# Feed forward's first batch: the low parts of weights and activations made by VectorE, between its decoding, with no work for GpSimd

## The chip, the core and the metric

The kernel runs on one core of a Trainium2 chip. The metric is the device time of one execution in microseconds. In this document TensorE does matrix products, VectorE and ScalarE work element by element, GpSimd is a fourth compute engine, and SyncE's queue (SP in the rows) starts the transfers from and to memory. In the rows they are called PE (PEld for its weight loads), DVE, ACT, POOL and SP.

## What is computed

Attention over 4 batches of 448 tokens with 12 heads, with a mixing of the heads before and behind the softmax; a feed forward of 768 to 2048 to 768; and then a layer of eight experts of which each token takes one. Cut to what matters here, the feed forward:

```python
def _moe_ref(x, w_in, w_out):            # x: 1792 x 768, w_in: 768 x 2048, w_out: 2048 x 768
    h = x @ w_in
    g = h * (1.0 / (1.0 + np.exp(-1.702 * h)))
    return (g @ w_out).astype(np.float32)
```

## The kernel before

TensorE multiplies numbers of a shortened format. To keep the accuracy of float32, each operand is split in two: a high part, the number rounded to that format, and a low part, the number less its high part. A product then takes three matmuls: high by high, high by low, low by high. ScalarE makes the high parts with a copy that rounds, and another engine makes the low parts with one subtraction.

The feed forward is the function `moe1`. It has 64 steps: 4 batches of tokens (b), and for each of them 16 slices (f) of 128 hidden columns. For a step the first layer (`l1`, line 268) runs 18 matmuls of 128x448, six blocks with three products each; the activation follows (`act`: tanh on ScalarE at line 273, then one instruction of VectorE at line 274; `act2`: the rounding copy on ScalarE at line 277 and the subtraction at line 278); and the second layer (`l2`, line 285) runs 18 matmuls that add to six sums.

The weights arrive in a form that VectorE has to decode first (`decode`, lines 251 to 254: four instructions of 128x768 for each tile of weights, with ScalarE's absolute value at line 246 for the last of them). The decoded weights stay in the core's memory, so decoding happens only in the first batch, two tiles in each of its steps 0 to 12 and one in step 13. The split of the weights (`split_w`, line 259 on ScalarE and line 260) is made anew for every batch.

The order of the instructions on every engine is the order of the program text. One step s of the loop issues, in this order: `act` of step s+1, `split_w` of the first layer's weights of s+2, `act2` of s+1, `split_w` of the second layer's weights of s+1, the decoding of the two tiles for the next step's splits, `l1` of s+2, and `l2` of s. In the middle of the decoding, behind each of its two instructions at line 253, the load of a tile for two steps later is issued; the very last load has one step. The buffers of the activations (`g`) are one for odd and one for even steps.

Which engine makes a low part: at line 260 GpSimd in the first batch and VectorE in the others, unless the caller names one; at line 278 always GpSimd. Some of the first steps' work (the list `EARLY`) is issued beside the end of the attention stage and names its engine itself. Between its steps the first batch also issues small setup instructions, most of them on GpSimd (`env.setup`, lines 444 to 459).

Of the kernel before, what the change touches and what calls it, by code (L numbers as in the profile page):

```python
# [6 lines left out]
F32 = mybir.dt.float32  # L7
# [4 lines left out]
ALU = mybir.AluOpType  # L12
# [188 lines left out]
def moe1(tc, env, x_in, w_in, w_out, wg):  # L201

    nc=env.nc; NF=FF//128; NE=5
    with ExitStack() as ctx, ExitStack() as late:
# [35 lines left out]
        def wtile(s,z):  # L240
            WS[s,z]=env.wsp.tile([128,2,DM],F32R,tag="ws",bufs=5,name="ws")
# [13 lines left out]
        def split_w(s,z,e=None):  # L255
            b,f=steps[s]; r=WR[f,z]
            if (s,z) not in WS: wtile(s,z)
            t=WS[s,z]
            nc.scalar.copy(t[:,0,:],r)  # L259
            (e or (nc.gpsimd if b==0 else nc.vector)).tensor_tensor(out=t[:,1,:],in0=r,in1=t[:,0,:].bitcast(F32),op=ALU.subtract)  # L260
        PSL={}
        def l1(s):
            b,f=steps[s]; ps=pl.tile([128,512],F32,tag="h",name="psh"); PSL[s]=ps; t=WS.pop((s,0))
# [11 lines left out]
        def act2(s):  # L275
            th=TH.pop(s)
            nc.scalar.copy(G[s][:,0,:],th)  # L277
            nc.gpsimd.tensor_tensor(out=G[s][:,1,:],in0=th,in1=G[s][:,0,:].bitcast(F32),op=ALU.subtract)  # L278
        def l2(s,between=lambda o:None):
            b,f=steps[s]; t=WS.pop((s,1)); g=G.pop(s)  # L280
            if f==0: OB[b]=[L.po.tile([128,512],F32,tag=f"o{o}",name=f"pso{o}") for o in range(6)]
            for i,o in enumerate((2,3,4,5,0,1)):
                between(i); c=slice(o*128,o*128+128)
                for k,(wz,xz) in enumerate(((0,0),(0,1),(1,0))):
                    nc.tensor.matmul(OB[b][o][:,:TB],t[:,wz,c],g[:,xz,:],start=f==0 and k==0,stop=f==NF-1 and k==2)  # L285
# [68 lines left out]
        def dk(*ks):  # L354
# [3 lines left out]
            if 3 in ks: nd[0]+=1  # L358
        A=lambda i: absd(*order[i])
        step={'a':lambda i: absd(*order[i]),'d':dk,'x':lambda c,e: split_x(0,c,EN[e]),'w':lambda s,z,e: split_w(s,z,EN[e]),'l':l1,'t':act,'u':act2}  # L360
        at=0; did=set()
        for t,k,a in EARLY:
# [11 lines left out]
        if ('u',0) not in did: act2(0)  # L374
        for s in range(NS):
            b,f=steps[s]
            if s+1<NS and ('t',s+1) not in did: act(s+1)
            if s+2<NS and ('w',s+2,0) not in did: split_w(s+2,0)
            if b>0 and f==0: evac(b-1)
            if s+1<NS and ('u',s+1) not in did: act2(s+1)  # L380
            if s+1<NS and ('w',s+1,1) not in did: split_w(s+1,1)
# [475 lines left out]
```

## Time and profile before

| | us |
|---|---|
| median of 3 runs | 1334.84 |
| the runs | 1334.59 to 1337.12 |
| the profiled execution | 1341.98 |
| span of the profiled execution | 1340.3 |

| over the span | busy us | share |
|---|---|---|
| TensorE | 1217.9 | 91% |
| VectorE | 787.0 | 59% |
| ScalarE | 606.5 | 45% |
| GpSimd | 312.7 | 23% |

The profile is that of one execution, and its times count from the start of its span. The shares are means over stages that differ: the attention fills about the first 470 us, the first batch of the feed forward lies between about 470 and 625 us, its other batches end at about 991 us, and the experts follow. The profiled execution takes 7.14 us more than the median of the runs, so a difference is worked out within the profile and then taken from the median.

### The profile page before, as it was taken

What the parts mean: (1) busy time and instruction counts of PE and PEld (TensorE: products, weight loads), DVE (VectorE), ACT (ScalarE), POOL (GpSimd) and SP (SyncE); (2) the same over time, 40 slices, a digit from 0 to 9 for tenths busy, and PEclk for the clock granted to TensorE, in tenths of its full rate; (3) what the DMA queues carried; (4) which work ended last, traced back from release to release, by engine and by line L of the source; (5) the groups of instructions that cost most, each with busy time, mean ns of one, the idle gap of its engine ahead of it and who ended that gap; (6) DMA issues with size and microseconds to landing.
All of it is one profiled execution on the core that took longest, in us unless ns stands there. A gap on an engine that the chain in (4) does not pass through costs nothing. (4 is left out here: it accounts for less than half of the span.)

```text
span 1340.3 us, 31619 instructions
## 1 busy us (share of the span) xinstructions
PE 1217.9 (91%) x13086; PEld 992.6 (74%) x13087; DVE 787.0 (59%) x1340; ACT 606.5 (45%) x1203; POOL 312.7 (23%) x385
## 2 busy tenths in 40 slices
PE   7798998898888788779999999999996979999996
PEld 2355555555555577668899899989996979999996
DVE  1565665565655799997543544454437645566663
ACT  2455555555554444434434433443334534445552
POOL 0111111111111555553121112112113202321110
PEclk9899999999999798989999999999997989999998
DMA  7887987987966355420100010000555756656500
GB/s 222 254 242 208 296 239 212 269 254 202 281 186 203 128 203 194 152 96 26 42 22 21 1 52 11 21 1 11 183 198 172 207 160 190 190 198 228 187 20 21
DMA packets 97825, 201.09 MB, mean 150 GB/s; under 512 B 29711, under 2 KB 67733, under 8 KB 97292
## 3 DMA queue, kind: packets, MB, share of 16 engines
q1 hardware_dynamic: 91596, 186.84, 45.4%
q0 software_dynamic: 6080, 12.18, 2.9%
q8 instruction: 104, 1.70, 0.5%
q14 instruction: 45, 0.37, 0.1%
HBM read 143.60 MB, written 56.43 MB: 149 GB/s over the span
## 5 line engine op out<-in xcount | busy, mean ns | idle before, releaser
L268 PE MATMUL psh<-x,ws 128*128 128x448 f32 x1152 | 264.1, 382 | 25.2 <-POOL ws L260 14.9
L268 PEld LDWEIGHTS psh<-x,ws 128*128 128x128 f32 x1152 | 224.5, 197 | 56.0 <-POOL ws L260 20.3
L285 PE MATMUL pso<-g,ws 128*128 128x448 f32 x1152 | 252.7, 369 | 0.0
L285 PEld LDWEIGHTS pso<-g,ws 128*128 128x128 f32 x1152 | 213.8, 188 | 20.1
L135 PEld LDWEIGHTS psa<-M,E 60*64 60x64 f32 x5760 | 98.2, 138 | 115.2 <-POOL M L126 103.7
L119 ACT ACTIVATE E<-psm,st 124x448 f32<-124x448 f32 x180 | 112.5, 629 | 127.3 <-DVE st L116 127.2
L126 POOL TENSOR_SCALAR M<-wq,st 124x60 f32<-124x60 f32 x180 | 78.7, 451 | 354.8 <-DVE st L123 270.1
L260 DVE TENSOR_TENSOR ws<-res,ws 128x768 fp32r<-128x768 f32 x81 | 91.4, 1128 | 105.8 <-ACT ws L259 102.8
L135 PE MATMUL psa<-M,E 60*64 60x60 f32 x5760 | 108.9, 224 | 48.7 <-POOL M L126 43.1
L278 POOL TENSOR_TENSOR g<-th,g 128x448 fp32r<-128x448 f32 x64 | 78.4, 1225 | 308.2 <-ACT g L277 308.1
L661 PE MATMUL psh<-xt,ws 128*128 128x256 f32 (+2 forms) x1152 | 147.7, 289 | 0.1
L661 PEld LDWEIGHTS psh<-xt,ws 128*128 128x128 f32 x1152 | 145.3, 190 | 0.3 <-DVE xt L653 0.3
L628 DVE TENSOR_TENSOR ws<-res,ws 128x768 fp32r<-128x768 f32 x128 | 121.9, 959 | 39.7 <-ACT ws L627 39.5
L143 DVE COPY AT<-psa 128x480 f32<-128x480 f32 x88 | 60.2, 685 | 133.1 <-ACT AT L142 133.1
L89 PE MATMUL psq<-K,Q 64*120 64x448 f32 (+1 forms) x384 | 114.8, 648 | 11.9 <-ACT so L94 7.0
L116 DVE TENSOR_REDUCE st<-psm 124x1 f32<-124x448 f32 x180 | 103.7, 617 | 14.6 <-PE psm L112 13.8
L680 PE MATMUL psy<-ws,hh 128*128 128x384 f32 x576 | 110.4, 345 | 0.0
L627 ACT CAST ws<-res 128x768 fp32r<-128x768 f32 x128 | 105.5, 832 | 7.9 <-PE psy L697 4.9
L259 ACT CAST ws<-res 128x768 fp32r<-128x768 f32 x108 | 89.9, 832 | 35.5 <-DVE res L254 35.5
L151 PE MATMUL psv<-AT,V 128*64 128x120 f32 (+1 forms) x1536 | 98.8, 273 | 6.9 <-DVE X L155 3.5
L680 PEld LDWEIGHTS psy<-ws,hh 128*128 128x128 f32 x576 | 100.9, 190 | 0.0
L112 PE MATMUL psm<-G,wp 60*64 60x448 f32 x720 | 94.5, 578 | 0.5 <-ACT E L119 0.5
(178 smaller groups left out, 1289.5 us busy)
## 6 DMA issues: line engine op xcount, KB each, us to landing
res<-in_wm SPq DMA_DIRECT2D x56, 768.0 KB
G<-S SPq DMA_DIRECT2D x176, 210.0 KB
S<-so SPq DMA_DIRECT2D x72, 420.0 KB
wd<-in_w_in SPq DMA_DIRECT2D x10, 768.0 KB
wd<-in_w_out SPq DMA_DIRECT2D x10, 768.0 KB
S<-so SPq DMA_DIRECT2D x24, 308.0 KB
V<-in_vT SPq DMA_DIRECT2D x16, 384.0 KB
K<-in_kT SPq DMA_DIRECT2D x11, 448.0 KB
```

Of the source, the lines that this page charges most:

```text
L89: nc.tensor.matmul(QP[t,p,z][:n],Q[t][r,p*n:p*n+n],K[b,p][0][r],start=True,stop=True)
L112: nc.tensor.matmul(PM[s,a][64*c:64*c+64],wp[r],G[s][r,c,:],start=True,stop=True)
L116: nc.vector.reduce_max(ST[s][:,0,a:a+1],PM[s,a][:124],axis=AX.X,negate=True)
L119: nc.scalar.activation(E[s,a],PM.pop((s,a))[:124],AF.Exp,bias=ST[s][:,0,a:a+1],scale=1.0,accum_out=ST[s][:,1,a:a+1])
L135: nc.tensor.matmul(PA[s][64*cp:64*cp+64,c,240*a+60*cc:240*a+60*cc+60],e[r,j:j+64],m[r],start=True,stop=True)
L151: for z in range(2): nc.tensor.matmul(ps[64*z:64*z+64,p%3,:n],V[b,2*p+z][:,j,:],AT[t][:,j,2*p+z,:n],start=j==0,stop=j==3)
L268: nc.tensor.matmul(ps[:,:TB],t[:,wz,c],x[:,xz,:],start=k==0,stop=k==17); k+=1
L285: nc.tensor.matmul(OB[b][o][:,:TB],t[:,wz,c],g[:,xz,:],start=f==0 and k==0,stop=f==NF-1 and k==2)
L627: nc.scalar.copy(t[:,0,:],r[:,c])
L628: nc.vector.tensor_tensor(out=t[:,1,:],in0=r[:,c],in1=t[:,0,:].bitcast(F32),op=ALU.subtract)
L661: nc.tensor.matmul(ps,w[:,a,k*128:(k+1)*128],x[:,b,:],start=k==0 and (a,b)==(0,0),stop=k==5 and a==1)
L680: nc.tensor.matmul(PY[e][2*c+z],h[:,a,c*CP:c*CP+CP],w[:,b,z*384:z*384+384],start=f==0 and k==0,stop=f==7 and k==2)
```

## The change

Two lines of `moe1` choose another engine. At line 260 the subtraction is now VectorE's in every batch (where the caller doesn't name another). At line 278 it is VectorE's for the steps 1 to 15, the rest of the first batch, and stays GpSimd's for step 0 and for the three later batches. Nothing else differs; the order of the program text is the same.

```diff
@@ split_w
             nc.scalar.copy(t[:,0,:],r)
-            (e or (nc.gpsimd if b==0 else nc.vector)).tensor_tensor(out=t[:,1,:],in0=r,in1=t[:,0,:].bitcast(F32),op=ALU.subtract)
+            (e or nc.vector).tensor_tensor(out=t[:,1,:],in0=r,in1=t[:,0,:].bitcast(F32),op=ALU.subtract)
@@ act2
             nc.scalar.copy(G[s][:,0,:],th)
-            nc.gpsimd.tensor_tensor(out=G[s][:,1,:],in0=th,in1=G[s][:,0,:].bitcast(F32),op=ALU.subtract)
+            (nc.vector if 0<s<16 else nc.gpsimd).tensor_tensor(out=G[s][:,1,:],in0=th,in1=G[s][:,0,:].bitcast(F32),op=ALU.subtract)
```

## Rows read from the trace of the kernel before

**Rows 1.** Stretches: length, busy time (instructions) by engine, granted clock, DMA share, GB/s.

```profile
480.04:608.12 128.08, 104.16 (x427) 87.90 (x428) 128.08 (x112) 51.60 (x73) 68.32 (x57) 0.89 0.41 149
...
636.72:991.00 354.28, 354.28 (x1779) 320.10 (x1778) 161.45 (x255) 147.07 (x254) 64.89 (x58) 1.00 0.14 48
```

**Rows 2.** Order of time, VectorE: start, length, engine, line, operation, tiles; two steps' first.

```profile
480.04 0.61 DVE L274 SCALAR_TENSOR_TENSOR th<-th,psh 128x448 f32<-128x448 f32 x1
...
608.12 0.61 DVE L274 SCALAR_TENSOR_TENSOR th<-th,psh 128x448 f32<-128x448 f32 x1
```

**Rows 3.** Order of time, one whole step; in brackets idle time before and its end.

```profile
564.67 0.84 ACT L259 CAST ws<-res 128x768 fp32r<-128x768 f32 x1 [2.10 <-DVE res L254]
565.43 0.60 DVE L274 SCALAR_TENSOR_TENSOR th<-th,psh 128x448 f32<-128x448 f32 x1
...
565.56 0.68 PE L268 MATMUL psh<-x,ws 128*128 128x448 f32 x2
565.65 1.82 POOL L260 TENSOR_TENSOR ws<-res,ws 128x768 fp32r<-128x768 f32 x1 [5.19 <-ACT ws L259]
565.96 3.37 DVE L251 TENSOR_SCALAR res<-res 128x768 int32<-128x768 int32 x2
566.12 0.56 ACT L277 CAST g<-th 128x448 fp32r<-128x448 f32 x1 [0.62 <-DVE th L274]
566.60 0.83 ACT L259 CAST ws<-res 128x768 fp32r<-128x768 f32 x1
...
567.43 1.49 POOL L278 TENSOR_TENSOR g<-th,g 128x448 fp32r<-128x448 f32 x1
...
567.53 3.50 PE L268 MATMUL psh<-x,ws 128*128 128x448 f32 x16 [1.29 <-POOL ws L260]
568.87 2.17 POOL L260 TENSOR_TENSOR ws<-res,ws 128x768 fp32r<-128x768 f32 x1
569.25 3.48 DVE L252 SCALAR_TENSOR_TENSOR res<-res 128x768 int32<-128x768 int32 x2
...
570.87 3.81 PE L285 MATMUL pso<-g,ws 128*128 128x448 f32 x18
...
572.65 1.81 DVE L253 SCALAR_TENSOR_TENSOR res<-res 128x768 int32<-128x768 int32 x2
...
574.39 1.81 DVE L254 SCALAR_TENSOR_TENSOR res<-wa,res 128x768 f32<-128x768 f32 x2
...
576.13 0.60 DVE L274 SCALAR_TENSOR_TENSOR th<-th,psh 128x448 f32<-128x448 f32 x1
```

**Rows 4.** Order of time, VectorE: instructions of these shapes outside the whole steps.

```profile
465.11 0.55 DVE L251 TENSOR_SCALAR re<-wd 128x768 int32<-128x768 int32 x1
...
472.24 2.67 DVE L251 TENSOR_SCALAR res<-wd 128x768 int32<-128x768 int32 x2
474.83 1.81 DVE L252 SCALAR_TENSOR_TENSOR res<-wd,res 128x768 int32<-128x768 int32 x2
...
615.95 0.95 DVE L260 TENSOR_TENSOR ws<-re,ws 128x768 fp32r<-128x768 f32 x1
616.82 3.30 DVE L228 TENSOR_TENSOR x<-xr,x 128x448 fp32r<-128x448 f32 x6
```

**Rows 5.** Order of time, TensorE: first layer of a step with the clock low.

```profile
522.78 0.68 PE L268 MATMUL psh<-x,ws 128*128 128x448 f32 x2 [1.65 <-ACT ws L259]
...
524.74 6.05 PE L268 MATMUL psh<-x,ws 128*128 128x448 f32 x16 [1.29 <-POOL ws L260]
```

**Rows 6.** Order of time: the last load, its decoding and the first layer behind it.

```profile
605.65 0.33 SPq L233 DMA_DIRECT2D wd<-in_w_out  x1
...
609.86 0.73 DVE L251 TENSOR_SCALAR res<-wd 128x768 int32<-128x768 int32 x1 [1.14 <-DMA wd<-in_w_out]
...
610.23 3.51 PE L268 MATMUL psh<-x,ws 128*128 128x448 f32 x16 [0.36 <-POOL ws L260]
```

**Rows 7.** Order of time, GpSimd: one setup instruction.

```profile
517.43 1.01 POOL L447 TENSOR_SCALAR_AFFINE_SELECT ident<-ident 128x128 f32<-128x128 f32 x1
```

## The prediction

> **What bounds the kernel now.** I read first the table of stretches [rows 1]. Its columns are the length of the stretch and then the busy time of each engine; the first row is twelve steps of the feed forward's first batch, the second most of the three batches behind it. In the second TensorE is busy for 354.28 of 354.28 us: that stage can't lose or gain by this change, and whatever the first batch gives up reaches it whole. In the first VectorE is busy for 128.08 of 128.08 us, TensorE for 104.16 at a granted clock of 0.89, GpSimd for 68.32. So VectorE sets the first batch, and at first sight the change brings work to the one engine that is full.
>
> Next the start of each step, which is the activation's VectorE instruction (line 274): the first of twelve whole steps starts at 480.04 and the one behind the twelfth at 608.12 [rows 2], so a step takes 128.08 / 12 = 10.67 us. The order of time of one step [rows 3] says what it is made of. VectorE runs without a gap: line 274 at 565.43, two of line 251 (3.37 us together), two of line 252 (3.48), two of line 253 (1.81), two of line 254 (1.81), and the next line 274 at 576.13. Lines 251 and 252 lie beside GpSimd's three instructions (565.65 for 1.82, 567.43 for 1.49, 568.87 for 2.17 us, that is up to 571.04); lines 253 and 254 start when GpSimd is done.
>
> Then the same lines where GpSimd does nothing beside them [rows 4]: line 251 takes 0.55 us, not 3.37 / 2 = 1.69, and a pair of line 252 takes 1.81 us, not 3.48. So of the step's 10.67 us, about (3.37 - 1.02) + (3.48 - 1.81) = 4.0 us is VectorE standing still in its own instructions while GpSimd works (1.02 is two of 0.55 less the overlap of 0.08 that neighbouring rows show). ScalarE is not the cause: its casts and VectorE's 253 and 254 go side by side at 1.81 a pair.
>
> **The change part by part.** It takes 27 subtractions of 128x768 (line 260) and 15 of 128x448 (line 278) from GpSimd and puts them into VectorE's queue, between line 274 and the decoding. Each of the twelve whole steps moves two of the first and one of the second; step 0 moves one of line 278 (its line 260 instructions were placed earlier and keep their engine), step 13 moves three, step 14 two.
>
> The new step, as starts after its line 274. Line 274 lets the next one start after 0.53 us [rows 3]. Line 260 on VectorE, beside no GpSimd work, takes 0.95 us, 0.87 to the next start; an instruction of line 278's shape takes (3.30 - 0.08) / 6 = 0.54 to the next start [rows 4]. What they wait for: the first cast ends at 565.51, 0.08 after line 274 starts, so the first line 260 goes at 0.53. Line 277's cast ends at 566.68, 1.25 after; line 278 comes up at 0.53 + 0.87 = 1.40 and goes at once. The second cast ends at 567.43, 2.00 after; the second line 260 comes up at 1.94 and goes at about 2.04, a wait of 0.10. It lets go at 2.91. Then the decoding unhindered: 1.00 for the pair of line 251, 1.73 for line 252 [rows 4], 1.74 each for 253 and 254 [rows 3]. Sum: 2.91 + 1.00 + 1.73 + 1.74 + 1.74 = 9.12 us. A step gives 10.67 - 9.12 = 1.55 us, twelve give 18.6.
>
> Bounds: without the wait the step is 9.02, twelve give 19.8; if each of the three subtractions loses 0.1 more to its cast's signal and line 251 takes the full 0.55 between starts, it is 9.4, and twelve give 15.2. I take 9.12, the rows as they stand.
>
> Behind the moved subtractions on VectorE stands the decoding, and behind that ScalarE's first cast of the next step; that is in the sum. What TensorE gets: the third matmul of line 268, the first that needs a low part, starts 2.10 us into the step now (567.53) and 0.53 + 0.95 + 0.05 = 1.53 us then. Its work is 0.68 + 3.50 + 3.81 = 7.99 us a step [rows 3], under 9.12, and the second layer would end at 1.53 + 3.50 + 3.85 = 8.9, 0.2 before the next step. Line 277's cast must wait for that end, because it overwrites what the second layer two steps before read (one buffer for each parity); it starts 0.70 into the step, so TensorE has 0.9 us in hand. The weight loads are issued in the middle of the decoding two steps before use; two shorter steps leave over 14 us, so nothing becomes late there. One load has a single step: issued at 605.65, it holds line 251 up by 1.14 us until 609.86 [rows 6], that is 4.2 us. Between the same two points VectorE will have 2.4 us more to do, so that wait vanishes.
>
> The ends. In step 13 line 268's third matmul starts at 610.23, 2.11 us after line 274, and from there TensorE runs almost without a gap; with 1.53 this gives 0.6 us more. In step 0 the pair of line 251 takes 2.67 us [rows 4], partly behind a GpSimd instruction that stays; line 278 comes in front and waits for its cast. I bound it by a gain of 1.0 (all its stall gone, the 0.54 added) and a loss of 0.5, and take 0.1. GpSimd's queue loses the work that held back its setup instructions, so these run close together at the start of the batch; the two longest are the affine selects, 1.01 us [rows 7] for one. They cost between nothing and 2.0 us, once; I take 0.2, near nothing, because each can hold VectorE only while it runs and only where VectorE's instruction comes second.
>
> Sum: 18.6 + 0.6 + 0.1 - 0.2 = 19.1 us. The profiled execution took 1341.98 us for a span of 1340.3, and the runs' median is 1334.84, 7.1 us less; the stage is a tenth of the span, so its gain differs by about a tenth of a microsecond between them. 1334.84 - 19.1 = 1315.7, and I say 1316.
>
> **The rivals.** *The full engine gets fuller (slower).* VectorE is busy in every microsecond of the stage [rows 1] and each step adds 0.87 + 0.54 + 0.87 + 0.10 = 2.4 us to its queue. If what stretches lines 251 and 252 isn't GpSimd but stays, all of it lands on the step: 12 x 2.4 = 28.6, which gives 1363 us. The point from which it decides: the change loses once less than 2.4 of the 4.0 us of stretch goes away. Against it: both lines are at their short times wherever GpSimd pauses, the pair of line 252 in the same loop one step before the first whole one [rows 4]. The Trainium skill speaks for this rival: "Perfetto Trace Analysis", section "Optimizing Scalar/DVE Operations", says that where VectorE is saturated, handing work to ScalarE or even GpSimd can make sense, and this change goes the other way; the same section adds that the two share a read port of SBUF, so that shifting work between them may not help, which would make the result about no change. The rows here say more than either: the sharing costs more than the work.
>
> *TensorE's clock eats a part.* In six of the twelve steps the granted clock falls to the lower level (1.2 GHz) for a while, which is why its mean is 0.89 [rows 1], and line 268's sixteen matmuls take about 5.0 us (four times) or 6.1 (twice), as at 524.74, in place of 3.5. Each time TensorE had stood idle both before the first two matmuls (1.65 us at 522.78) and again before the third (1.29) [rows 5]. A seventh step with both gaps kept its clock, and in the five with the second gap at most, as in [rows 3], it never fell. Today VectorE's slowness covers these dips. If six came as now, the second layer would end 1.5 or 2.6 us later, past the 0.9 in hand, and line 277 and all behind it on VectorE would slip by 0.6 or 1.7: 4 x 0.6 + 2 x 1.7 = 5.8 us, giving 1321.5. Against it: the gaps shrink to 0.4 and 0.7 us, together less than the one gap that never brought a dip.
>
> *The gain is given back later.* Something behind the batch that runs by its own time (a load, a table in memory) would keep TensorE waiting: 1335 us. Against it: TensorE is busy for all of the second row of [rows 1], and the last weight load of the stage is issued in its step 12, which moves with it.
>
> **How the numbers follow.** Forecast 0.80, at 1316, with its own range of 1314 to 1320 from the bounds on the step and the ends; the clock 0.11, at 1321.5; given back 0.04; fuller engine 0.05. A measurement of this kernel can tell about 0.2%, 2.7 us, from no change. Faster 0.80 + 0.11 = 0.91, same 0.04, slower 0.05. The range takes in the forecast's and the clock's: 1313.5 to 1322.
>
> **What would show it.** In the changed profile, VectorE's lines 251 and 252 in the batch at 0.55 and 0.96 us each; line 260 at 0.95 and line 278 near 0.6 on VectorE; starts of line 274 9.1 us apart; TensorE's clock near 1.00 all through the stage; no wait of line 251 for a load. I am wrong if lines 251 and 252 keep over 1.5 us, if line 277 is seen waiting for the second layer in many steps, or if TensorE shows new gaps behind the first batch.

## The result, and the profile after

The changed kernel takes 1314.58 us (median, 1313.85 to 1316.98) beside 1335.98 for the kernel before in the same comparison: a ratio of 0.984 with a 95% interval of 0.9825 to 0.9856, or 21.4 us less. The forecast was 1316, 19 us less.

The profiled execution has a span of 1313.2 us, 27.1 less than the one of before, and not all of that is the change. Line 274's first start in the stage lies at 465.34 and no longer at 471.70: 6.36 us come from the attention ahead of it, which the change doesn't touch; over the runs below that leave the attention as it is, the same start lies anywhere from 464.03 to 468.60. From there to the start that stood at 636.72 before and stands at 609.82 now, the stage takes 144.48 us in place of 165.02: **20.54 us**. Behind it 0.2 us are left. The 20.5 of the profile and the 21.4 of the runs agree within the interval.

The table of stretches of the changed kernel answers [rows 1]: twelve whole steps, the end of the first batch, the batches behind.

```profile
473.46:582.21 108.75, 94.50 (x432) 79.25 (x432) 108.54 (x147) 51.62 (x73) 0.00 (x0) 1.00 0.49 175
582.21:609.82 27.61, 26.74 (x131) 24.47 (x132) 19.93 (x29) 14.78 (x28) 2.31 (x2) 1.00 0.04 16
609.82:964.00 354.18, 354.18 (x1778) 320.00 (x1777) 161.45 (x255) 146.96 (x254) 64.78 (x58) 1.00 0.14 48
```

The twelve steps take 108.75 us in place of 128.08, so 9.06 a step. VectorE is nearly as full as before (108.54 of 108.75) although it now does GpSimd's work as well; GpSimd does nothing; TensorE's granted clock is 1.00 in place of 0.89. The batches behind take 354.18 us, as before. One step in order of time answers [rows 3]:

```profile
518.77 0.62 DVE L274 SCALAR_TENSOR_TENSOR th<-th,psh 128x448 f32<-128x448 f32 x1
...
518.91 0.68 PE L268 MATMUL psh<-x,ws 128*128 128x448 f32 x2 [0.50 <-ACT ws L259]
519.30 0.95 DVE L260 TENSOR_TENSOR ws<-res,ws 128x768 fp32r<-128x768 f32 x1
...
519.95 0.83 ACT L259 CAST ws<-res 128x768 fp32r<-128x768 f32 x1
520.17 0.62 DVE L278 TENSOR_TENSOR g<-th,g 128x448 fp32r<-128x448 f32 x1
...
520.31 3.58 PE L268 MATMUL psh<-x,ws 128*128 128x448 f32 x16 [0.73 <-DVE ws L260]
...
520.81 0.96 DVE L260 TENSOR_TENSOR ws<-res,ws 128x768 fp32r<-128x768 f32 x1
521.69 1.02 DVE L251 TENSOR_SCALAR res<-wd 128x768 int32<-128x768 int32 x2
522.62 1.82 DVE L252 SCALAR_TENSOR_TENSOR res<-wd,res 128x768 int32<-128x768 int32 x2
...
524.36 1.82 DVE L253 SCALAR_TENSOR_TENSOR res<-wd,res 128x768 int32<-128x768 int32 x2
...
526.10 1.82 DVE L254 SCALAR_TENSOR_TENSOR res<-wa,res 128x768 f32<-128x768 f32 x2
...
527.84 0.62 DVE L274 SCALAR_TENSOR_TENSOR th<-th,psh 128x448 f32<-128x448 f32 x1
```

The reader is to see three things. The pairs of lines 251 and 252 take 1.02 and 1.82 us, not 3.37 and 3.48. The three moved subtractions stand ahead of them with 0.95, 0.62 and 0.96. And TensorE's third matmul starts 1.54 us into the step (520.31 less 518.77), where it was 2.10. The list of line 251 and of line 252 from the batch's third step on (least, median and largest length in ns) shows that no instruction is stretched there any more; the other half of the tiles has 551/552/556 and 947/950/953.

```profile
L251 DVE TENSOR_SCALAR res<-wd x13: 552/554/556, 485.4 to 585.1; 128x768 int32<-128x768 int32 x13
...
L252 DVE SCALAR_TENSOR_TENSOR res<-wd,res x13: 949/952/958, 486.4 to 585.7; 128x768 int32<-128x768 int32 x13
```

### The profile page after: what moved, and what is told of

It is laid out like the page before. It is cut to its first block, busy times and chain, and to the rows that moved or that the text cites. A ratio compares the mean times of both kernels' runs of the same rounds, so it can differ in the third digit from the quotient of the medians.

```text
span 1313.2 us, 31593 instructions
## 1 busy us (share of the span) xinstructions
PE 1204.8 (92%) x13086; PEld 981.9 (75%) x13087; DVE 767.1 (58%) x1382; ACT 606.3 (46%) x1203; POOL 236.9 (18%) x343
## 5 line engine op out<-in xcount | busy, mean ns | idle before, releaser
L268 PE MATMUL psh<-x,ws 128*128 128x448 f32 x1152 | 252.8, 371 | 15.7 <-DVE ws L260 9.5
L268 PEld LDWEIGHTS psh<-x,ws 128*128 128x128 f32 x1152 | 215.2, 189 | 45.1 <-DVE ws L260 14.4
L260 DVE TENSOR_TENSOR ws<-res,ws 128x768 fp32r<-128x768 f32 x108 | 117.1, 1084 | 106.2 <-ACT ws L259 102.9
L628 DVE TENSOR_TENSOR ws<-res,ws 128x768 fp32r<-128x768 f32 x128 | 121.8, 958 | 40.5 <-ACT ws L627 40.5
L278 POOL TENSOR_TENSOR g<-th,g 128x448 fp32r<-128x448 f32 x49 | 56.6, 1155 | 428.3 <-ACT g L277 428.2
```

Source lines behind the costliest of these rows:

```text
L260: (e or nc.vector).tensor_tensor(out=t[:,1,:],in0=r,in1=t[:,0,:].bitcast(F32),op=ALU.subtract)
L268: nc.tensor.matmul(ps[:,:TB],t[:,wz,c],x[:,xz,:],start=k==0,stop=k==17); k+=1
L628: nc.vector.tensor_tensor(out=t[:,1,:],in0=r[:,c],in1=t[:,0,:].bitcast(F32),op=ALU.subtract)
```

## The experiments

The question for the chip was whether GpSimd's presence stretched VectorE's decoding (the theory of the prediction) or whether the gain came from somewhere else: the low parts reaching TensorE earlier, or the chain through GpSimd. "Step" is the mean distance of line 274's starts over the twelve whole steps, in one profiled execution; the chips of the comparisons differ, so steps, and ratios to the kernel before on the same chip, are what is compared. Where a kernel has lines added, its line numbers are one or two higher. A kernel without a ratio was run once, and only its profile is used.

| kernel | step, us | ratio to before (95%) |
|---|---|---|
| before | 10.67 | |
| the whole change | 9.06 | 0.984 (0.9825 to 0.9856) |
| line 260 alone | 9.47 | 0.9873 (0.9857 to 0.989) |
| line 278 alone | 10.32 | 0.9967 (0.9953 to 0.9982) |
| change, spare subtractions on GpSimd | 12.94 | |
| change, spare copies on GpSimd | 10.37 | |
| change, one more subtraction on VectorE | 9.93 | |
| change, line 251 ahead of the second line 260 | 8.95 | |
| before, GpSimd only fills | 7.08; 7.30 in the last six | |

**One part alone: line 260.** The edit is shown against the changed kernel, as are the others unless said.

```diff
-            (nc.vector if 0<s<16 else nc.gpsimd).tensor_tensor(out=G[s][:,1,:], ...
+            nc.gpsimd.tensor_tensor(out=G[s][:,1,:], ...
```

> One part of the change alone: line 260 (the weights' low parts) goes to VectorE, line 278 (the activation's) stays with GpSimd. My theory (whole instructions of VectorE that read two tiles, or use both of its ports, stand still while a reading GpSimd instruction runs): GpSimd's one instruction a step starts some 1.3 us into the step and takes 1.15 us, so VectorE's second line 260 waits for it until about 2.5. Step 9.4 to 9.7 us, twelve steps give 12 to 15 us against the kernel before, and about 6 us less than the whole change. Rival (the gain comes from the low part reaching TensorE earlier, 1.5 us into the step and not 2.1): this part alone brings that, so nearly the whole gain, step 9.06 or, as VectorE has 0.54 us less of its own work, 8.5.

The step is 9.47, as my theory had it. The order of time of one step:

```profile
533.54 0.61 DVE L274 SCALAR_TENSOR_TENSOR th<-th,psh 128x448 f32<-128x448 f32 x1
...
534.89 1.15 POOL L278 TENSOR_TENSOR g<-th,g 128x448 fp32r<-128x448 f32 x1 [7.36 <-ACT g L277]
...
535.08 3.57 PE L268 MATMUL psh<-x,ws 128*128 128x448 f32 x16 [0.72 <-DVE ws L260]
...
535.58 1.28 DVE L260 TENSOR_TENSOR ws<-res,ws 128x768 fp32r<-128x768 f32 x1 [0.56 <-ACT ws L259]
...
536.78 1.02 DVE L251 TENSOR_SCALAR res<-res 128x768 int32<-128x768 int32 x2
```

GpSimd's instruction runs to 536.04, VectorE's line 260 beside it takes 1.28 in place of 0.96, and line 251 behind it is at its short time. The rival of the earlier low part falls: TensorE's third matmul starts 1.54 us into the step here too (535.08 less 533.54), as in the whole change, and the step is 0.41 longer. The step also shows why line 278's own work costs next to nothing in the whole change. The second line 260 starts 2.04 us into the step in both kernels, when ScalarE's second cast is done; here VectorE stands idle for 0.56 us before it, and there it makes line 278 in that time.

**The other part alone: line 278.**

```diff
-            (e or nc.vector).tensor_tensor(out=t[:,1,:],in0=r, ...
+            (e or (nc.gpsimd if b==0 else nc.vector)).tensor_tensor(out=t[:,1,:],in0=r, ...
```

> The other part alone: line 278 goes to VectorE, line 260 stays with GpSimd. My theory: VectorE's line 278 waits until GpSimd's first line 260 ends (2.04 us into the step), GpSimd's second one then holds the first line 251 until about 4.4; step about 10.5 us, within 0.3 of before, gain 0 to 4 us. So the parts don't add up in proportion to the work moved: GpSimd has to be out of the stretch. Rival (each microsecond taken from GpSimd gives its share): line 278 is a quarter of GpSimd's time, so a quarter of the gain, 5 us, step 10.25. Rival (VectorE is full, its own work counts): step 10.67 + 0.54 = 11.2, 6 us slower.

The step is 10.32. That is nearer to the first rival's 10.25 than to my 10.5, and the second rival (11.2) is out. My sentence that the parts would not add up is wrong: the two parts alone give 1.20 and 0.35 us of the step, together 1.55 of the whole change's 1.61, and the ratios say the same, 17 and 4.4 us against 21.4. What I had missed stands in the step:

```profile
546.61 4.02 POOL L260 TENSOR_TENSOR ws<-res,ws 128x768 fp32r<-128x768 f32 x2 [5.75 <-ACT ws L259]
...
547.69 1.23 DVE L278 TENSOR_TENSOR g<-th,g 128x448 fp32r<-128x448 f32 x1 [0.69 <-ACT g L277]
...
548.84 2.68 DVE L251 TENSOR_SCALAR res<-wd 128x768 int32<-128x768 int32 x2
...
551.45 1.81 DVE L252 SCALAR_TENSOR_TENSOR res<-wd,res 128x768 int32<-128x768 int32 x2
```

Only line 278 (0.6 us) and the pair of line 251 (1.66) are stretched now, line 252 no longer; and 0.69 us of GpSimd's time lies beside VectorE's wait for line 277, where it holds nothing.

**GpSimd does the subtractions once more, for nobody.**

```diff
+            if e is None and b==0: nc.gpsimd.tensor_tensor(out=L.du,in0=r,in1=t[:,0,:].bitcast(F32),op=ALU.subtract)
...
+            if 0<s<16: nc.gpsimd.tensor_tensor(out=L.du[:,:TB],in0=th,in1=G[s][:,0,:].bitcast(F32),op=ALU.subtract)
```

> The changed kernel, and besides GpSimd makes the same 42 subtractions once more, into a tile that nobody reads. My theory: with nobody waiting for them, they still hold VectorE: GpSimd's instructions of 1.8, 1.15 and 1.8 us, of which 0.3 lie beside line 274 that doesn't mind, add about 4.5 us; step 13 to 13.6 us, twelve steps 47 to 55 us over the changed kernel. Rival (GpSimd's place in the chain was the cost: VectorE and TensorE waited for its results): step stays at 9.06.

```profile
539.09 1.82 POOL L261 TENSOR_TENSOR du<-res,ws 128x768 bf16<-128x768 f32 x1 [7.11 <-ACT ws L259]
539.40 2.32 DVE L260 TENSOR_TENSOR ws<-res,ws 128x768 fp32r<-128x768 f32 x1
...
540.99 1.75 POOL L280 TENSOR_TENSOR du<-th,g 128x448 bf16<-128x448 f32 x1
541.65 1.57 DVE L279 TENSOR_TENSOR g<-th,g 128x448 fp32r<-128x448 f32 x1
...
542.82 2.09 POOL L261 TENSOR_TENSOR du<-res,ws 128x768 bf16<-128x768 f32 x1
543.15 2.58 DVE L260 TENSOR_TENSOR ws<-res,ws 128x768 fp32r<-128x768 f32 x1
```

This settles the cause. Nobody reads what GpSimd makes here, and yet the step is 12.94 us, 3.88 over the changed kernel (my range began at 13.0). The rival with the chain, 9.06, falls. VectorE is busy in every microsecond of the twelve steps, without an instruction more than in the changed kernel (147):

```profile
474.18:629.40 155.22, 116.51 (x432) 97.72 (x432) 155.22 (x147) 51.36 (x73) 71.77 (x57) 0.82 0.34 123
```

VectorE's three subtractions end 0.81, 0.48 and 0.82 us behind GpSimd's, one after the other: the first starts at 539.40, GpSimd's runs to 540.91, and VectorE's ends at 541.72 after 2.32 us in place of 0.95.

**The same with spare copies, which read one tile.** In both added lines `tensor_tensor` becomes a copy of the high part.

> As the run with GpSimd's spare subtractions, but each is a spare copy that reads one tile (the high part) and not two. It asks whether a reading GpSimd instruction holds VectorE whatever it computes. My theory (it holds for its own time): a copy of 768 takes 0.8 to 1.1 us, one of 448 0.5 to 0.7; the first lies partly beside line 274, which doesn't mind; step 9.06 + 0.5 + 0.5 + 0.9, some 10.5 to 11.3 us. Rival (only two-tile GpSimd instructions hold VectorE): step 9.06 to 9.2.

```profile
545.23 0.82 POOL L261 CAST du<-ws 128x768 bf16<-128x768 f32 x1 [7.00 <-ACT ws L259]
545.49 1.37 DVE L260 TENSOR_TENSOR ws<-res,ws 128x768 fp32r<-128x768 f32 x1
...
547.42 1.03 POOL L261 CAST du<-ws 128x768 bf16<-128x768 f32 x1
547.68 1.57 DVE L260 TENSOR_TENSOR ws<-res,ws 128x768 fp32r<-128x768 f32 x1
```

The step is 10.37, 1.31 over the changed kernel, a little under my 10.5 to 11.3. The rival falls: copies that read one tile hold VectorE too: its line 260 takes 1.37 us in place of 0.95 and ends 0.81 behind the copy.

**VectorE gets one more subtraction in each step.**

```diff
+            if 0<s<13: nc.vector.tensor_tensor(out=du,in0=WR[0,0],in1=WR[1,0],op=ALU.subtract)
             dec()
```

> The changed kernel with one more subtraction of 128x768 on VectorE ahead of the decoding in each of the steps 1 to 12, into a tile that nobody reads. My theory: VectorE alone still sets the step, so each microsecond counts: step 9.06 + 0.87 = 9.93, 10.4 us over the changed kernel, TensorE's two idle gaps longer by 0.87 in sum; it may then see the low clock again in some steps, hidden by VectorE. Rival (the stage is now bound by TensorE and the waits for it, 7.99 us of work and 1.1 of waiting): part of the 0.87 is hidden, step under 9.6.

The step is 9.93, the 9.06 + 0.87 of the theory to the hundredth: VectorE's queue alone sets the changed step, and a microsecond put into it costs a microsecond. So the rival of the full engine was right in its premise. It was wrong on what filled the engine.

**Line 251 ahead of the second line 260.** The decoding's first instruction for both tiles goes ahead of `split_w(s+1,1)`, so that the wait for ScalarE's second cast has work in front of it.

> The changed kernel with the pair of line 251 moved ahead of the second line 260, so that the wait for ScalarE's second cast (0.09 us a step) has work in front of it. My theory (VectorE's queue alone sets the step, every gap in it counts): step 9.06 - 0.09 = 8.97, 1.1 us less over twelve steps, too little for the time and seen in the starts of line 274 only. Rival (something else sets the step by now): stays at 9.06.

The step is 8.95, 0.11 less. That is 1.3 us over the twelve steps, the same reading from the other side; a gain of this size was looked for in the step alone.

**The kernel before with GpSimd only filling.** GpSimd's subtractions of the first batch become fills with zero (the edit is against the kernel before).

```diff
+            if e is None and b==0: nc.gpsimd.memset(t[:,1,:].bitcast(F32),0.0)
...
+            if 0<s<16: nc.gpsimd.memset(G[s][:,1,:].bitcast(F32),0.0)
```

> The kernel before, with GpSimd's 27 + 15 subtractions of the first batch replaced by fills with zero of the same tiles (the low parts of that batch's weights and activations are left out): GpSimd writes, but reads nothing. It asks which GpSimd instruction holds VectorE. My theory (a reading one holds it): the pair of line 252 falls to 1.82 us, the pair of line 251 lies between 1.0 and 2.5 (it writes through both ports), VectorE needs under 8.3 us, TensorE's 8.0 us then set the step: 8.0 to 8.6. Rival (any busy GpSimd instruction stretches VectorE in proportion): with fills of about half the time, about 2 of the 4 us of stretch stay on lines 251 and 252 both, VectorE needs 8.7 and the pair of line 252 stays over 2.4.

The step settles at 7.30, less than either theory had. In the first six steps VectorE is full and they take 6.68 to 7.15; in the last six TensorE is, and they take 7.30 each (all twelve: 7.08). The table of stretches, for the first six steps and the last six:

```profile
475.62:516.76 41.14, 41.01 (x202) 38.03 (x203) 41.14 (x56) 25.06 (x37) 18.17 (x20) 1.00 0.70 259
516.76:560.54 43.78, 43.78 (x217) 40.58 (x217) 41.38 (x57) 25.16 (x37) 13.65 (x37) 1.00 0.53 186
```

So TensorE's work is 7.30 us a step: its rows overlap, and the 7.99 us that I had added up from them counted some time twice. The order of time in step 1 and in a later step:

```profile
475.29 1.42 POOL L260 MEMSET ws<- 128x768 f32 x2
...
476.16 1.43 DVE L251 TENSOR_SCALAR res<-res 128x768 int32<-128x768 int32 x2
...
527.27 1.82 DVE L253 SCALAR_TENSOR_TENSOR res<-wd,res 128x768 int32<-128x768 int32 x2
...
527.65 0.74 POOL L260 MEMSET ws<- 128x768 f32 x1
...
528.46 0.74 POOL L260 MEMSET ws<- 128x768 f32 x1
```

A fill reads nothing. Line 253, which reads two tiles, takes 1.82 a pair beside two fills, its time alone. Line 251, with one input and a result in the core's memory, takes 1.43 beside one, 0.41 more than alone. So a fill holds line 251 but not line 253, and the rival (any busy GpSimd stretches in proportion) falls. The Trainium skill, "SBUF — State Buffer", section "Who interferes with whom", tells it so: GpSimd and VectorE share one pair of ports, an instruction of VectorE with two inputs there collides with GpSimd's reads and not with its writes, and one in a mode that uses both ports collides with GpSimd as well. The rows of line 253 agree. Those of line 251 agree if it runs in such a mode, which no run here shows by itself; it takes 0.55 us for as many elements as line 252 does in 0.95.

**Does it carry to the attention?**

```diff
-            nc.gpsimd.tensor_scalar_mul(M2[s,a],wq,st[:,3,a:a+1])
+            nc.vector.tensor_scalar_mul(M2[s,a],wq,st[:,3,a:a+1])
```

> The changed kernel, and in the attention stage the mixing weights (line 126, 124x60, 180 times, 0.43 us each on GpSimd) go to VectorE too. It asks whether the lesson carries to a place where VectorE is not full. There GpSimd's instruction is a link of a chain that TensorE waits for (95.9 us of waiting of its weight loads for line 126 in the profile after), and VectorE has about a third of the time free. My theory: on VectorE the instruction takes under 0.2 us and needs one signal less, so the attention stage gets shorter, by 0 to 25 us, 10 as the middle: 1290 to 1315. Rival (VectorE's queue is in order, and line 126 falls behind evictions of 0.6 us that wait for TensorE): slower, by up to 20 us.

The rival was right: the ratio to the kernel before is 0.9983 (0.9968 to 0.9999) in place of the changed kernel's 0.984, so this edit gives back about 1.4%, some 19 us, by ratios from two chips. The loss lies in the attention: line 274's first start behind it is at 486.27 us, where no other run here has it later than 471.70, and the feed forward's steps are 9.09 us, nearly as in the changed kernel. Line 126 takes 0.25 us on VectorE and not under 0.2. The sums of waiting in the attention (us in total, times, longest), first of the changed kernel from 50 to 440 us, then of this one from 50 to 460:

```profile
ACT E L119 <- DVE st L116: 120.6, 88, 2.8
PEld psa L135 <- POOL M L126: 95.9, 84, 3.0
...
PE psa L135 <- POOL M L126: 35.5, 49, 2.1
```

```profile
ACT E L119 <- DVE st L116: 172.2, 88, 3.6
...
PE psa L135 <- DVE M L126: 52.5, 70, 3.9
```

TensorE's matmuls of line 135 wait longer for line 126, 52.5 us in place of 35.5, and not less, as I had hoped. Their weight loads no longer wait for line 126 (95.9 before), but 58.1 us for line 94 on ScalarE and 58.9 for nothing that the profile shows. ScalarE's exponentials wait 51.6 us more for VectorE's maximum (line 116), which now stands behind line 126 in VectorE's queue. VectorE is busy for 262.68 of 410 us there, so it isn't full. That its place in the order is what costs, and that these waits are the whole loss, is argued from the sums and was not shown by a run.

## Why the prediction was right

The forecast's mechanism held, and its working goes through the profile term by term:

- *The step.* 9.12 us were worked out, 9.06 came. Every term but one is met within 0.02: the second line 260 waits 0.09 (0.10), the third matmul starts at 1.53 (1.53), the pairs of lines 252 to 254 take 1.73 or 1.74. The pair of line 251 was put at 1.00 to the next start and takes 0.94, as the prediction's own rows had it (1.02 less the overlap of 0.08); the prediction gives no reason for 1.00. Twelve steps give 19.3 us, not 18.6.
- *The ends.* For the end of the batch 0.6 us was put down, and 0.99 came (27.61 in place of 28.60). The start of the third matmul gave 0.57, as expected. The rest lies in places where I had not looked, two short waits of TensorE in the kernel before that are gone. One, of 0.24 us by the starts around it, is the same hold: GpSimd's last line 260 held one of VectorE's that TensorE needed. The other, 0.18, is a wait for line 228, which came late behind the last tile's decoding. In order of time of the kernel before:

```profile
617.50 3.34 PEld L268 LDWEIGHTS psh<-x,ws 128*128 128x128 f32 x17 [0.29 <-DVE x L228]
...
622.50 1.86 POOL L260 TENSOR_TENSOR ws<-res,ws 128x768 fp32r<-128x768 f32 x1
...
623.41 1.77 DVE L260 TENSOR_TENSOR ws<-re,ws 128x768 fp32r<-128x768 f32 x1
...
625.24 3.14 PEld L268 LDWEIGHTS psh<-x,ws 128*128 128x128 f32 x16 [0.35 <-DVE ws L260]
```

- *Step 0 and the setup.* Step 0 takes 8.12 us in place of 8.34. GpSimd's setup instructions do run in one bunch there; the pairs of lines 251 and 252 take 1.12 and 1.89, 0.17 over the other steps, where 0.2 was put down. Together a gain of 0.22 where 0.1 less 0.2 had been counted.
- *The load of one step's lead.* The wait of 1.14 us [rows 6] is gone, as said.
- *The sum.* 19.33 + 0.99 + 0.22 = 20.54, the stage's difference. 19.1 was forecast; of the 1.4 that it was short, the pair of line 251 is 0.7, the end of the batch 0.4 and step 0 with the setup 0.3. That the total came so near rests on the steps; the ends were small guesses, and all three errors lie on the same side.
- *The rivals.* The full engine is answered by the spare subtractions on either engine: VectorE is the bound, and GpSimd's work was dearer for it than its own. The clock stayed at 1.00 in all twelve steps, with gaps of TensorE of 0.4 to 0.6 and 0.73 us. The other runs show that the gaps alone don't decide a fall. In the part with line 260 alone, gaps of 0.82 and 0.73 us came before a fall in one step (the sixteen matmuls of line 268 take 5.09 us at 563.25, at a granted clock of 0.66) and before none in the step ahead of it (3.51 at 553.85, 1.00), and gaps of 1.20 and 0.72 before none either (3.57 at 535.08). With GpSimd's spare subtractions the clock fell once with the second gap alone (2.11 us, then 5.09 at 580.62). So the prediction's tie to both gaps doesn't hold, and why the clock stayed up in the changed kernel is open. The rival's way to the time is real but smaller than its price. The run with line 126 on VectorE has the changed kernel's feed forward, and there the clock fell once, in the first whole step. Line 277 then waited for the second layer, and the next step took 9.29 us in place of 9.06, so a fall that made line 268's matmuls 1.3 us longer cost 0.23, where 0.6 was put down for one of 1.5:

```profile
496.10 4.82 PE L268 MATMUL psh<-x,ws 128*128 128x448 f32 x16 [0.74 <-DVE ws L260]
...
504.61 0.57 ACT L277 CAST g<-th 128x448 fp32r<-128x448 f32 x1 [0.89 <-PE pso L285]
```

- *The rival of the gain given back.* Nothing was given back later: the batches behind take the same 354 us.
- *Wrong in the text, without a price.* TensorE's work is not 7.99 us a step but 7.30.

## What to carry to other kernels

When one engine is busy all of the time, compare each of its instructions with the same instruction at a place where its neighbour rests, before you move work away from it: a stretched instruction counts as busy, and 4.0 of 10.67 us were such. Work on GpSimd that reads the core's memory beside a full VectorE cost VectorE about half to three quarters of the time that GpSimd was shown busy with it: 4.0 us a step for 5.5 in the kernel before, 3.88 for 5.7 with the spare subtractions, 1.31 for 2.75 (0.82, 0.90 and 1.03) with the spare copies. Taking it back paid here because VectorE does it in less, 2.3 us a step to the next start. In the attention, where VectorE is not full, the same step lost.

## What the runs showed of the hardware

- The hold is nearly whole: VectorE's subtraction of 128x768 that came second ended 0.81 us behind GpSimd's instruction, in both runs with spare work on GpSimd (541.72 after 540.91, 546.86 after 546.05), where alone it takes 0.95. So all but 0.14 us of its time falls behind GpSimd's end.
- The two take turns: with spare subtractions, GpSimd's line 280 takes 1.75 us in place of 1.15, because VectorE's line 260 was before it.
- The hold goes the other way too, and for longer than one instruction: in the run with fills, GpSimd's affine select of 128x128, which reads a tile, starts at 499.17 beside VectorE's lines 252 to 254 and takes 4.18 us, up to 503.35, where it takes 0.66 in step 0 of the changed kernel. VectorE's pairs keep their 1.81.
- A GpSimd fill holds the instruction with one input (line 251, 1.43 a pair and not 1.02) and leaves the one with two inputs alone (line 253, 1.82).
